# RWKV-7 recurrence and GELU MLP: the first five chunks as an explicit order of small steps, one PSUM place per product, and 64x128 tiles in three more chunks

## The chip, the cores and the metric
The kernel runs on one core of a Trainium2 chip. The metric is the device time of one execution in microseconds (us). Five engines work side by side, each through its own instructions in order: TensorE (PE in the profile; its weight loads are PEld), VectorE (DVE), ScalarE (ACT), GpSimd (POOL) and SyncE (SP), which only issues DMAs. DMAs are issued on the queues of SyncE (SPq), ScalarE (ACTq) and GpSimd (POOLq).

## The reference
A recurrence over 768 steps, for 4 batches and 8 heads with a 40 x 40 state each, feeds a two-layer MLP with the exact GELU over all 3072 tokens:

```python
for t in range(S):                                   # S = 768, D = 40
    kt, vt, rt = (k[:, :, t], v[:, :, t], r[:, :, t])
    wt, at, bt = (w[:, :, t], a[:, :, t], b[:, :, t])
    y[:, :, t] = np.einsum('bhd,bhde->bhe', rt, state)
    Sa = np.einsum('bhde,bhe->bhd', state, at)
    state = (state * wt[:, :, None, :] - np.einsum('bhd,bhe->bhde', Sa, bt)
             + np.einsum('bhd,bhe->bhde', vt, kt))

x = y.transpose(0, 2, 1, 3).reshape(B * S, H * D)    # 3072 x 320
h = x @ w_in                                         # 320 x 2048
g = 0.5 * h * (1.0 + erf(h * inv_sqrt2))
out = g @ w_out                                      # 2048 x 320
```

The two weights reach the kernel as 64-bit floats, and are made into 32-bit floats on the chip.

## The kernel before
**The recurrence in chunks.** The 768 steps are cut into 12 chunks of 64. Inside a chunk the recurrence is solved with matrix products. A chunk c goes through these functions (the tile names are those of the profile): `logs`, `sums` and `turn_w` make the running decays (tiles wT, cum); `turn_a`, `turn_b`, `turn_k`, `turn_v`, `turn_r` transpose the inputs on TensorE, and `scale_a`, `scale_b`, `scale_k` apply the decays. `make_N` multiplies the scaled a and b (N_ps) and masks the product into N, `make_A` and `make_RV` do the same for their products. The unit triangular matrix of N is inverted. Then X is what the state gives (`make_X`), sa what the chunk's steps write back (`make_saT`, `make_sa`, tile SM), M and QY the two parts of the output (`make_M`, `make_y2`, `make_QY`), xt the chunk's 128-row input to the MLP (`outputs`), and `new_state` makes the next state.

**The inverse** of chunk 0 is found by repeated squares on TensorE (`squares`, five of them). From chunk 1 on it goes through GpSimd: `make_N` stores the 32 x 32 blocks of N to DRAM with four DMAs on SyncE, `start_inverse` loads them as Nb with two, its 31 column steps (two instructions each, L759 and L761, or st/spare_x in chunk 1, W/tmp from chunk 2 on) eliminate, `store_inverse` writes the blocks back, `fetch_inverse` loads them as Tt and T2. `turn_corner` transposes one of them, `corner` makes the off-diagonal product J and copies it to Js, `joined` makes the second product (J too in the profile) and copies it into Tt. From chunk 5 on Nb comes from a transpose on VectorE (`turn_N`) instead of DRAM.

**The MLP.** `mlp(c)` is a generator of pieces. Eight products "ph" (two in each of four PSUM tiles; L1167) multiply xt with w_in, a GELU on ScalarE moves each PSUM tile into gt (L1169), and "po" multiplies gt with w_out: plainly for chunks 0 to 2 (L1178), with seven products of half the size in place of eight from chunk 3 on (`seven`, L1098). A ph product goes in 64x64 tiles or, for chunks 3 to 8, in 64x128 tiles.

**Weights.** `first_load(False, part)` brings a quarter of the raw w_in words (1.05 MB), `first_load(True, part)` the last rows of a half (0.52 MB), `second_load(f, ...)` a sixteenth of w_out (0.33 MB). The conversion of a piece (`to_float`, in generator form, 10 for w_in and 16 for w_out) is some eight instructions over VectorE, ScalarE and GpSimd or VectorE. `convert(n)` issues the first half of n pieces and the second half of the pieces begun before.

**Order.** The schedule is written out by hand: the order of the source lines is the order in which each engine issues. For the first chunks it is a list of calls (L1227 to L1485), then a loop `for c in range(3, NCH)` in which `fill()` places the next piece of an MLP between the steps of the recurrence. A call such as `make_N(c)` there issues its matmuls, and its mask or copy right behind them. PSUM is four places of two banks ("duo0" to "duo3"); `places` gives each product its place in the order of the calls. `keep(n, ...)` puts n columns of 128 (ident times the mask cum_m) in front of the next product, as work that only keeps TensorE busy; a call replaces what an earlier one asked for and no product has taken yet, and so 12 such columns are issued. `unused(tile, eng)` fills the unused rows of an input tile with a constant before its load.

```python
    ("ph", "123322000100030003000300030003000300030003001302"),
    ...
def duo(name):
    pt = psum.tile([P, 2, 512], FP32, tag="duo" + next(places[name]), name=name, bufs=1)
    while asked:
        n = asked.pop()
        mm(pt[:, 0, :n * P], ident, cum_m.unsqueeze(1).to_broadcast([P, n, P]))
    return pt
```

Of the kernel before, what the change touches and what calls it, by code (L numbers as in the profile page):

```python
# [20 lines left out]
def kernel(  # L21
# [49 lines left out]
    P = 128  # L71
# [22 lines left out]
    def keep(*columns):  # L94
# [3 lines left out]
    places = {n: iter(x) for n, x in (  # L98
        ("warm", "0"),
        ("wT_ps", "30112"),  # L100
        ("cum", "22031"),
        ("aT_ps", "200"),
        ("nT_ps", "0313"),
        ("N_ps", "310322222222"),
        ("sq", "20332"),
        ("kT_ps", "1033"),
        ("A_ps", "312000000000"),
        ("vT_ps", "012"),
        ("rT_ps", "122"),
        ("RV_ps", "020111111111"),  # L110
        ("J", "133022222222"),
        ("av", "310010000000"),
        ("QY", "200121212323232323232323"),
        ("J2", "213322222222"),
        ("sap", "333"),
        ("saT_ps", "200321111111"),
        ("M_ps", "023311111111"),
        ("X", "20211111111"),
        ("tn_ps", "32"),
        ("ph", "123322000100030003000300030003000300030003001302"),  # L120
        ("po", "133130313031303130313031303130313021302"),
    )}
# [124 lines left out]
    def load_VR(c):  # L247
        VR = turned_in.setdefault(c, {})["VR"] = VR_ring()
        for e in range(2):
            nc.sync.dma_start(out=VR[half(e)].rearrange("p g q m d -> p (g q m) d")[:, :, :D], in_=rows_of(v, c, e))  # L250
# [20 lines left out]
    st_ring = ring("st", 1, [P, 2, NP, G, HP], lambda t: t.rearrange("p e i g d -> p (e i g) d")[:, :, D:], nc.gpsimd)  # L271
    SM_ring = ring("SM", 1, [P, 2, G, NP, VC], None, None)
    early_b = work.tile([P, NK, TB], FP32, tag="xt", name="early_b").rearrange("p k t -> p (k t)")
    early_w = SM_ring().rearrange("p e g n c -> p (e g n c)")[:, :G * DM + REST]
# [76 lines left out]
    def to_float(dst, words, eng):  # L351


        n = words.shape[1] // 2
        lo, hi = (words.rearrange("p (n x) -> p n x", x=2)[:, :, x] for x in range(2))
        both = work.tile([P, LW], UINT32, tag="conv", name="conv", bufs=2)
        power, mant = both[:, :n], both[:, LW // 2:LW // 2 + n]
        nc.vector.tensor_scalar(power, hi, 0x7FF00000, None, ALU.bitwise_and)  # L358
        nc.scalar.activation(power, power, ACT.Relu, bias=rebias, scale=8.0)  # L359
        nc.vector.tensor_scalar(mant, hi, 0x000FFFFF, 0x00100000, ALU.bitwise_and, ALU.bitwise_or)  # L360
        if eng is nc.vector:
            yield
        nc.vector.scalar_tensor_tensor(power, hi, 0x80000000, power, ALU.bitwise_and, ALU.bitwise_or)
        mant_f, power_f, lo_f = mant.bitcast(FP32), power.bitcast(FP32), lo.bitcast(FP32)
        if eng is nc.vector:
            eng.scalar_tensor_tensor(mant_f, lo, 2.0 ** -32, mant, ALU.mult, ALU.add)
            eng.scalar_tensor_tensor(dst, mant_f, 2.0 ** -20, power_f, ALU.mult, ALU.mult)
        else:
            nc.scalar.mul(lo_f, lo, 2.0 ** -52)
            nc.scalar.mul(mant_f, mant, 2.0 ** -20)  # L370
            eng.tensor_tensor(mant_f, mant_f, lo_f, ALU.add)
            eng.tensor_tensor(dst, mant_f, power_f, ALU.mult)
        yield

    queue, begun = [], []

    def convert(n, last=False):

        for _ in range(n):
            begun.append(queue.pop(0))  # L380
            next(begun[-1], None)
            if len(begun) > 1:
                next(begun.pop(0), None)
        if last:
            while begun:
                next(begun.pop(0), None)
# [40 lines left out]
    def first_convert(kt, part, eng):  # L427
        if wide_in:
            w = LW // 2
            yield from to_float(w_in_sb[:, kt, part * w:(part + 1) * w], first_raw.pop((kt, part)), eng)  # L430

# [13 lines left out]
    def second_convert(f, eng):  # L445
        if wide_out:
            yield from to_float(w_out_sb[:, f], second_raw.pop(f), eng)

    def first_pieces(kts, part, eng):
        queue.extend(first_convert(kt, part, eng) for kt in kts)  # L450

    def second_pieces(engs):
        queue.extend(second_convert(f, {"v": nc.vector, "g": nc.gpsimd}[e]) for f, e in enumerate(engs))
# [6 lines left out]
    decays, turned_in = {}, {}  # L460
# [5 lines left out]
    def sums(c):  # L466
        logw = raws.pop((c, "w"))
        pt = duo("wT_ps").rearrange("p e (n t) -> p e n t", t=C)
# [5 lines left out]
        cum = duo("cum")[:, :, :DM]  # L474
# [4 lines left out]
        wp = wp_ring()  # L479
        turned_in.setdefault(c, {})["wp"] = wp  # L480
        if c < NB:
            nc.scalar.activation(wp[:, :, 1:].rearrange("p (n e) t -> p e n t", e=2), pt, ACT.Exp)  # L482
        else:
            en = turned_in.setdefault(c, {})["en"] = by_batch(side("en", "kT", 1))
            for to, scale_ in ((wp[:, :, 1:].rearrange("p (g n e) t -> p g e n t", g=G, e=2), 1.0),
                               (en.rearrange("p (e g n) t -> p g e n t", e=2, g=G), -1.0)):
                for g in range(G):
                    nc.scalar.activation(to[:, g], pt[:, ::1 - 2 * g, g * NP:(g + 1) * NP], ACT.Exp, scale=scale_)
        rw = (avs_ring if c in (1, 2) else part_ring)()[:, :, :DM]
# [3 lines left out]
    def turn_w(c):  # L493
        wp = turned_in.setdefault(c, {})["wp"] = wp_of[(c - NB - 1) % 3]
# [28 lines left out]
    def flip(src, name):  # L523

        pt = duo(name).rearrange("p g (n t) -> p g n t", n=NP)
# [21 lines left out]
    def turn_a(c):  # L547
        if c < NT:
            turned_in.setdefault(c, {})["a_ps"] = flip(by_pair(raws.pop((c, "a"))), "aT_ps")
            return  # L550
        aT = turned_in.setdefault(c, {})["aT"] = work.tile([P, 2, G, NP, C], FP32, tag="aT", name="aT", bufs=2)
# [33 lines left out]
    def turn_b(c):  # L585
        t = turned_in[c]
        nT = side("nT", "nT", 1)
        if c >= NB:
            nT = by_batch(nT)
# [4 lines left out]
        nc.scalar.copy(nT, flip(by_pair(t["nb"]), "nT_ps"))  # L594
# [8 lines left out]
    def turn_k(c):  # L603
        t = turned_in[c]
        if c >= NB:
            kT = t["k_turned"] = by_batch(side("k_turned", "conv", 2))
            turn(kT, c, "k_turned")
            return
        kT = side("kT", "kT", 1)
        nc.scalar.copy(kT, flip(by_pair(t["ks"]), "kT_ps"))  # L610
# [8 lines left out]
    def turn_v(c):  # L619
        t = turned_in[c]  # L620
        vT = side("vT", "late", 1)
        if c < NT:
            pt = duo("vT_ps").rearrange("p q (m t) -> p q m t", m=NP)
            for q in range(2):
                for m in range(NP):
                    for g in range(G):
                        mm(pt[half(g), q, m], t["VR"][:, g, q, m, :HP], ident)
            nc.scalar.copy(vT, pt)
        else:
            turn(vT.rearrange("p q m (e t) -> p (q m e) t", e=2), c, "v")  # L630
        t["vT"] = parts(vT)

    def turn_r(c):
        rT = side("rT", "rT", 2)
        if c < NT:
            raw = raws.pop((c, "r"))
            nc.scalar.copy(rT, flip(lambda q, m: raw[:, NP * q + m].rearrange("p g d -> p (g d)"), "rT_ps"))
        else:
            turn(rT.rearrange("p q m (e t) -> p (q m e) t", e=2), c, "r")
# [11 lines left out]
    def products(name, lT, rT, swap):  # L651

        pt = duo(name).rearrange("p j (g n t) -> p j g n t", g=G, n=NP)
# [18 lines left out]
    def make_N(c):  # L672
# [9 lines left out]
        masked(flat(N), products("N_ps", t["nT"], t["aT"], True))  # L682
        if c > NB:
            for q in (1, 3):
                rows = slice(q * BL, (q + 1) * BL)
                nc.scalar.copy(flat(N)[rows, :, :BL], flat(N)[rows, :, BL:])  # L686
        if c in direct or c > NB:
            return
# [8 lines left out]
    def make_RV(c, mask=True):  # L697
        t = turned_in[c]
        t["RV_ps"] = products("RV_ps", t["vT"], t["rT"], False)
        if mask:  # L700
            mask_RV(c)

    def mask_RV(c):
# [4 lines left out]
        else:  # L708
            nc.scalar.copy(to, t.pop("RV_ps"))
            nc.gpsimd.tensor_tensor(to, to, upper.unsqueeze(1).to_broadcast([P, 2 * G * NP, C]), ALU.mult)  # L710

    def make_A(c, mask=True):
        t = turned_in[c]
        t["A"] = work.tile([P, 2, G, NP, C], FP32, tag="nT", name="A")
        t["A_ps"] = products("A_ps", t["kT"], t["aT"], False)
        if mask:
            mask_A(c)
# [5 lines left out]
    def make_av(c):  # L723
        t = turned_in[c]
        av = duo("av")[:, :, :G * NP * D].rearrange("p x (g i d) -> p x g i d", g=G, i=NP)
        for g, i, x, e, q, m in units():
            mm(av[half(e ^ x), x, g, i], t["A"][half(e), x, g, i], t["VR"][half(e), g, q, m, :D])
        avs = t["avs"] = avs_ring()
        nc.scalar.copy(avs[:, :, :DM], av.rearrange("p x g i d -> p x (g i d)"))
# [4 lines left out]
    def start_inverse(c, eng, place=None):  # L734
# [10 lines left out]
        for y in range(2 if c > NB else 0):  # L745
            eng.tensor_copy(W.rearrange("p s t -> p (s t)")[:, y::BL + 2][:, :BL // 2],
# [934 lines left out]
```

## Time and profile before

| | |
|---|---|
| runs, us | 673.82, 674.12, 674.56 |
| span of the profiled execution, us | 673.1 |
| granted TensorE clock over the span | 0.964 |
| PE busy | 634.4 us, 94% of the span, 14602 matmuls |
| PEld busy | 550.9 us, 82% |
| DVE busy | 430.0 us, 64% |
| POOL busy | 403.9 us, 60% |
| ACT busy | 329.8 us, 49% |
| DMA | 70.11 MB, 104 GB/s on average |

The span runs from the first to the last recorded instruction of one execution; the profile gives no other time for that execution, and its span lies 1.0 us under the median of the runs. A PE row such as "101.27 4.48 PE L1167 MATMUL ph<-xt,w_in_sb 64*64 64x256 f32 x77" in the time-ordered view reads: start at 101.27 us, 4.48 us long, 77 matmuls of line 1167 in 64x64 tiles over 256 columns. A bracket behind it gives the idle time before it and what ended it. The slices are 16.8 us long.

### The profile page before, as it was taken

How to read it: one execution, taken by the hardware profiler on the slowest of the kernel's cores; microseconds unless marked ns; L12 is line 12 of the kernel's file. 1: busy time of each engine (PE TensorE's matmuls, PEld its weight loads, DVE VectorE, ACT ScalarE, POOL GpSimd, SP SyncE). 2: the span in 40 equal slices, each digit the busy share in tenths (PEclk: the TensorE clock that was granted, in tenths of full speed). 3: DMA queues.
4: the chain of work that ended last, by engine and by line, in shares of the span. 5: the costliest groups of instructions: out<-in, count | busy, mean ns of one | idle time of the engine just before them, and what ended most of it. 6: DMA issues, size and time to landing. Idle time of an engine off the chain costs nothing.

```text
span 673.1 us, 32696 instructions
## 1 busy us (share of the span) xinstructions
PE 634.4 (94%) x14602; PEld 550.9 (82%) x14602; DVE 430.0 (64%) x571; ACT 329.8 (49%) x637; POOL 403.9 (60%) x835
## 2 busy tenths in 40 slices
PE   7668888879999999999999999999999999999997
PEld 4557767666777787899899899898998998989977
DVE  2322869996435596787887887696887865623303
ACT  5223565362332562673772855845737728344020
POOL 5648327870581586876886877868868868720000
PEclk9785789899999999999999999999999999999999
DMA  9777747946745855726748648557457471220100
GB/s 136 140 147 124 125 90 181 186 82 127 150 97 99 155 111 98 132 60 112 131 88 134 127 79 135 117 93 151 99 96 137 93 124 42 50 50 4 41 2 21
DMA packets 270607, 70.11 MB, mean 104 GB/s; under 512 B 251003, under 2 KB 267675, under 8 KB 270466
## 3 DMA queue, kind: packets, MB, share of 16 engines
q1 hardware_dynamic: 265146, 62.10, 49.9%
q0 software_dynamic: 1680, 4.07, 3.4%
q8 instruction: 115, 1.88, 1.2%
q10 hardware_dynamic: 3640, 1.84, 1.1%
q14 instruction: 26, 0.21, 0.1%
HBM read 56.16 MB, written 7.86 MB: 95 GB/s over the span
## 4 chain that ended last, share of the span: by engine, by line
PE 80%; DVE 9%; POOL 4%; issue 2%; ACT 2%; DMA 1%; ACTq 1%; SPq 0%; DVEq 0%; POOLq 0%
PE ph L1167 28%; PE po L1098 21%; PE po L1178 8%; PE QY L138 6%; PE J L138 2%; PE X L138 2%; POOL st L761 2%; POOL st L759 2%; PE A_ps L138 2%; PE N_ps L138 1%; PE saT_ps L138 1%; PE av L138 1%; PE RV_ps L138 1%; PE M_ps L138 1%; PE sq L138 1%
## 5 line engine op out<-in xcount | busy, mean ns | idle before, releaser
L1167 PE MATMUL ph<-xt,w_in_sb 64*64 64x256 f32 (+1 forms) x2896 | 218.3, 377 | 1.3 <-ACT gt L1169 1.2
L1167 PEld LDWEIGHTS ph<-xt,w_in_sb 64*64 64x64 f32 (+1 forms) x2896 | 170.4, 151 | 33.5 <-ACT gt L1169 1.9
L759 POOL TENSOR_TENSOR tmp<-W,Nb 128x126 f32<-128x126 f32 (+22 forms) x310 | 130.3, 420 | 62.1 <-DMA Nb<-N 39.1
L761 POOL TENSOR_TENSOR W<-W,tmp 128x126 f32<-128x126 f32 (+22 forms) x310 | 140.5, 453 | 24.3
L1098 PE MATMUL po<-w_out_sb,gt 128*128 128x160 f32 x576 | 82.7, 302 | 0.3 <-issue 0.3
L1098 PEld LDWEIGHTS po<-w_out_sb,gt 128*128 128x128 f32 x576 | 78.8, 190 | 1.7 <-issue 0.6
L1169 ACT ACTIVATE gt<-ph 128x1024 f32<-128x1024 f32 x48 | 49.2, 1024 | 43.3 <-PE ph L1167 42.7
L1066 ACT COPY turned<-within 32x256 f32<-32x256 f32 (+3 forms) x144 | 46.4, 322 | 26.3 <-DVE within L1055 24.5
L1178 PE MATMUL po<-w_out_sb,gt 128*128 128x320 f32 x192 | 55.8, 448 | 2.2 <-ACT wpT L482 2.2
L1178 PEld LDWEIGHTS po<-w_out_sb,gt 128*128 128x128 f32 x192 | 36.7, 195 | 17.4 <-ACT wpT L482 2.4
L961 ACT COPY SM<-sa 32x64 f32<-32x64 f32 (+1 forms) x108 | 31.9, 295 | 14.0 <-DVE sa L955 12.4
L521 ACT COPY part<-part 32x256 f32<-32x256 f32 (+1 forms) x112 | 36.1, 322 | 1.5
L1102 DVE TENSOR_TENSOR os<-os,po 128x160 f32<-128x160 f32 x63 | 20.0, 318 | 24.0 <-PE po L1098 20.9
L359 ACT ACTIVATE conv<-conv,rebias 128x320 uint32<-128x320 uint32 (+1 forms) x26 | 16.1, 624 | 35.3 <-DVE conv L358 28.7
L886 ACT COPY Js<-J 128x256 f32<-128x256 f32 x11 | 4.1, 371 | 56.6 <-PE J L138 56.6
L710 POOL TENSOR_TENSOR VR<-VR,upper 128x1024 f32<-128x1024 f32 x8 | 19.0, 2370 | 17.8 <-DMA Tt<-inv 11.1
L955 DVE STREAM_TRANSPOSE sa<-saT 128x1024 f32<-128x1024 f32 x9 | 11.2, 1242 | 26.3 <-ACT saT L945 26.3
L1098 PE MATMUL po<-extra,half 128*128 128x160 f32 x176 | 26.1, 303 | 0.0
L686 ACT COPY N<-N 32x512 f32<-32x512 f32 x14 | 8.6, 616 | 34.8 <-DVE N L649 34.7
L1098 PEld LDWEIGHTS po<-extra,half 128*128 128x128 f32 x176 | 24.2, 190 | 0.3
L1118 DVE TENSOR_TENSOR half<-gt 128x1024 f32<-128x1024 f32 x9 | 11.4, 1265 | 18.3 <-ACT gt L1169 18.3
L1011 DVE TENSOR_TENSOR xt<-QY,wpT 128x512 f32<-128x512 f32 x18 | 11.5, 682 | 16.9 <-PE QY L138 16.9
(257 smaller groups left out, 1203.2 us busy)
## 6 DMA issues: line engine op xcount, KB each, us to landing
VR<-in_v_dram SPq DMA_DIRECT2D x24, 160.0 KB
out_dram<-os SPq DMA_DIRECT2D x46, 80.0 KB
b_rows<-in_b_dram SPq DMA_DIRECT2D x22, 160.0 KB
k_rows<-in_k_dram SPq DMA_DIRECT2D x22, 160.0 KB
Tt<-inv SPq DMA_DIRECT2D x44, 64.0 KB
a_pairs<-in_a_dram SPq DMA_DIRECT2D x18, 144.0 KB
v_pairs<-in_v_dram SPq DMA_DIRECT2D x36, 72.0 KB
r_pairs<-in_r_dram SPq DMA_DIRECT2D x36, 72.0 KB
```

The lines of the kernel that those rows point to most:

```text
L138: nc.tensor.matmul(o, lhsT, rhs, start=first, stop=True, skip_group_check=True)
L521: nc.scalar.copy(to[at:at + BL, :, x, z * BL:end], tmp[on:on + BL, e, :, q * BL:q * BL + end - z * BL])
L710: nc.gpsimd.tensor_tensor(to, to, upper.unsqueeze(1).to_broadcast([P, 2 * G * NP, C]), ALU.mult)
L759: eng.tensor_tensor(t, W[:, :rows, j:j + 1].to_broadcast([P, rows, rest]), Nb[:, j:j + 1, j + 1:].to_broadcast([P, rows, rest]), ALU.mult)
L761: eng.tensor_tensor(W[:, :rows, j + 1:], W[:, :rows, j + 1:], t, ALU.add)
L961: copy(t["SM"][to:to + BL, g].rearrange("p q m c -> p (q m) c")[:, :, d * BL:end], t["sa"][at:at + BL, :, to:to + end - d * BL])
L1066: nc.scalar.copy(tn[to:to + deep, :, at:at + wide], within[0][at:at + deep, :, to:to + wide])
L1098: nc.tensor.matmul(po[:, n, :DM // 2], l_[:, f], r_[:, f], start=f == 0, stop=f == NF // 2 - 1)
L1102: nc.vector.tensor_tensor(to, one_, other, ALU.add)
L1167: nc.tensor.matmul(ph[to:end, x, s, g], w_in_sb[half(x), kt, p * P + to:p * P + end], xt[half(x), kt, g], start=kt == 0, stop=kt == NK - 1)
L1169: nc.scalar.activation(gt[:, 4 * q:4 * q + 4].rearrange("p (x s) t -> p x s t", x=2), ph, ACT.Gelu)
L1178: nc.tensor.matmul(po[:, g], gt[:, f, g * P:(g + 1) * P], w_out_sb[:, f], start=f == 0, stop=f == NF - 1)
```

## The change
It rewrites how the first five chunks are ordered, and three details.

- Functions that issued matmuls and the copies or masks behind them are cut into parts that are called one by one: `make_N`, `mask_N`, `store_N`; `start_inverse`, `load_Nb`, `substitute` (n column steps); `flip_v`, `copy_v` and the like; `corner`, `copy_corner`; `joined`, `copy_joined`; `make_X`, `add_X`; `square(k)`, `turn_square(k)`; `scale_y`, `move_y`; `ph`, `gelu`, `po`, `put` for the MLP. A conversion becomes a `Unit` with the steps a, r, m, b, s, g, each for one engine (a, m, b on VectorE, r and s on ScalarE, g on GpSimd).
- The order of chunks 0 to 4 is one long list of such steps; the loop begins at c = 5 and there takes the same steps in the same order as before.
- `duo(name, at)` takes the PSUM place by the chunk or product, no longer by the order of calls, and the table is a new one for the first chunks.
- 72 columns of `keep` are issued in place of 12.
- ph goes in 64x128 tiles in chunks 0 to 8. In chunk 2 one product was split into column halves; it no longer is.
- The w_out loads that were issued on ScalarE's queue (3, 4, 8, 9, 11) are issued on SyncE's.
- The state's tile (st) and SM become single tiles instead of rings where they were ones of one.

```diff
-    def duo(name):
-        pt = psum.tile([P, 2, 512], FP32, tag="duo" + next(places[name]), name=name, bufs=1)
+    def duo(name, at):
+        pt = psum.tile([P, 2, 512], FP32, tag="duo" + places[name][at], name=name, bufs=1)
...
-        ("N_ps", "310322222222"),
+        ("N_ps", "203132022222"),
...
-        ("ph", "123322000100030003000300030003000300030003001302"),
+        ("ph", "122200013020032201000100030003000300030003001302"),
...
+    class Unit:
+        def a(self):
...
+            nc.vector.tensor_scalar(self.power, self.hi, 0x7FF00000, None, ALU.bitwise_and)
+        def r(self):
+            nc.scalar.activation(self.power, self.power, ACT.Relu, bias=rebias, scale=8.0)
+        def m(self):
+            nc.vector.tensor_scalar(self.mant, self.hi, 0x000FFFFF, 0x00100000, ALU.bitwise_and, ALU.bitwise_or)
...
+    def substitute(c, n=BL):
+        run(islice(steps_of[c], n))
...
-                        for to, end in ((0, P),) if NS <= c < NCH - 3 and q in (0,1,2,3,) else ((0, HP), (HP, P)):
+                for to, end in ((0, P),) if c in wide_chunks else ((0, HP), (HP, P)):
...
+    phs, pos, wide_chunks = {}, {}, range(NCH - 3)
```

The list around the three steps that the prediction follows. Chunk 1 before, from the store of N (inside `make_N(1)`) to the load of Nb (inside `start_inverse(1)`), and after:

```diff
-    make_N(1)
-    scale_k(0)
...
-    first_load(False, 0, early(0, 4), eng=nc.gpsimd)
-    run(zero)
-    run(start_inverse(1, nc.gpsimd, (spare_x[:, :BL * BL], spare_w[:, :nw], spare_w[:, nw:])))
...
-    first_load(True, 0, early(4), eng=nc.sync)
-    corner_direct(0, (nc.scalar, nc.scalar, nc.scalar, nc.scalar))
-    make_av(0)
-    first_load(False, 1, eng=nc.sync)
+    first_load(False, 0, early(0, 4), eng=nc.gpsimd)
+    first_load(False, 1, eng=nc.sync)
+    keep(1, 4)
+    make_N(1)
+    mask_N(1)
+    load_VR(1)
+    keep(1, 4)
+    square(1)
+    mask_A(0)
+    store_N(1)
+    U[0].a()
...
+    turn_square(1)
...
+    first_load(True, 1, spare_raw[:, :LW], eng=nc.sync)
...
+    start_inverse(1, nc.gpsimd, (spare_x[:, :BL * BL], spare_w[:, :nw], spare_w[:, nw:]))
+    load_Nb(1)
+    substitute(1, 8)
```

From chunk 1's corner to chunk 2's column steps:

```diff
-    corner(1)
...
-    make_X(1)
...
-    joined(1)
...
-    make_sa(1)
...
-    make_N(2)
-    convert(1)
-    convert(1)
-    fill()
-    run(start_inverse(2, nc.gpsimd))
-    for n in "av": unused(paired[n], nc.gpsimd, 1.0)
+    make_X(1)
...
+    turn_corner(1)
+    corner(1)
...
+    joined(1)
+    copy_joined(1)
...
+    make_N(2)
+    mask_N(2)
+    store_N(2)
+    ph(0, 0)
...
+    load_Nb(2)
+    load_w(3)
...
+    load_a(3)
...
+    unused(paired['a'], nc.gpsimd, 1.0)
+    logs(3)
+    substitute(2, 8)
```

Around chunk 2's corner and joined, which stands behind them on TensorE:

```diff
-    corner(2)
-    load_v(3)
-    fill()
...
-    turn_b(3)
-    make_X(2)
-    make_N(3)
-    seconds(1, (14, 14), last=True)
-    run(start_inverse(3, nc.gpsimd))
-    load_r(3)
-    joined(2)
+    po(0, 0, 0)
...
+    make_X(2)
...
+    po(0, 1, 0)
...
+    make_N(3)
...
+    corner(2)
+    copy_corner(2)
+    keep(2)
+    joined(2)
+    copy_joined(2)
+    mask_N(3)
```

More of the change, by code (lines that the diff above doesn't have):

```diff
@@ L1190 @@
-    pieces = []
-    def fill(n=1):
-        while n and pieces:
-            if next(pieces[0], "end") == "end":
-                pieces.pop(0)
-            else:
-                n -= 1
-    def load_next(c):
-        load_w(c)
-        load_a(c)
-    def seconds(n, *loads, last=False):
-        convert(n, last)
-        for load in loads:
-            second_load(*load)
+            ph(c, q)
+            gelu(c, q)
+            yield
+        yield from seven(c)
+    sevens = {c: seven(c) for c in (3,)}
@@ new lines @@
+    turn_w(6)
+    load_a(6)
+    turn_corner(4)
+    put(2, 0)
+    corner(4)
+    load_VR(5)
+    copy_corner(4)
+    store_inverse(5, (nc.gpsimd,))
+    make_X(4)
+    weight_sums(1)
+    joined(4)
+    gelu(3, 2)
+    turn_blocks(range(0, 8))
+    put(2, 1)
+    turn_k(5)
+    turn_part(5, ())
+    ph(3, 3)
+    copy_joined(4)
+    add_X(4)
+    keep(1)
+    make_saT(4)
+    copy_saT(4)
+    gelu(3, 3)
+    start_inverse(6, nc.gpsimd)
+    ph(3, 1)
+    gelu(3, 1)
+    substitute(5, 8)
+    substitute(5, 8)
@@ L1563 @@
[L1563 to L1565 removed]
             if more2:
                 turn_r(n2)
[L1568 to L1570 removed]
                 scale_a(n2)
[L1572 to L1573 removed]
+            else:
+                scale_kT(n)
+        next(pieces)
+        if more:
             turn_part(n, range(10, 16))
             scale_b(n, nc.gpsimd)
[L1576 removed]
+            substitute(n)
```

1480 lines of the change are left out of this document (893 added, 587 removed).

## The prediction
> **What bounds the kernel now.** I read the page's slices first, then busy time by stretch, then the time-ordered rows of TensorE, of SyncE's DMA queue and of GpSimd around the first three chunks. The slices:
>
> ```profile
> PE   7668888879999999999999999999999999999997
> PEclk9785789899999999999999999999999999999999
> ```
>
> Left of slice 10 (168 us) TensorE is neither full nor at full clock; right of it there is nothing to win except by doing less work. Busy time by stretch (us, then TensorE, weight loads, VectorE, ScalarE, GpSimd, granted clock, DMA share, GB/s):
>
> ```profile
> 0.00:40.00 40.00, 27.13 (x754) 20.73 (x757) 11.72 (x14) 15.07 (x17) 19.09 (x49) 0.91 0.84 138
> 40.00:80.00 40.00, 32.87 (x979) 29.65 (x972) 18.60 (x24) 16.58 (x24) 27.51 (x66) 0.66 0.71 126
> 80.00:120.00 40.00, 33.37 (x1000) 29.47 (x999) 31.16 (x44) 22.83 (x32) 19.71 (x28) 0.90 0.65 144
> 120.00:160.00 40.00, 33.98 (x645) 25.36 (x638) 35.72 (x69) 18.14 (x25) 25.53 (x58) 0.93 0.68 135
> 160.00:200.00 40.00, 38.62 (x947) 29.87 (x945) 17.12 (x32) 13.73 (x17) 21.56 (x57) 1.00 0.61 123
> ```
>
> TensorE idles 32.7 us up to 160 and 1.4 us up to 200. Its busy time below full clock (27.13 x 0.09 + 32.87 x 0.34 + 33.37 x 0.10 + 33.98 x 0.07) is 19 us more. So 53 us is all that a new order can ever win. TensorE's rows show where the loss ends:
>
> ```profile
> 101.27 4.48 PE L1167 MATMUL ph<-xt,w_in_sb 64*64 64x256 f32 x77
> ...
> 154.43 0.75 PE L138 MATMUL J<-L,N 32*32 32x32 f32 x64
> 155.11 4.57 PE L1178 MATMUL po<-w_out_sb,gt 128*128 128x320 f32 x16
> ...
> 161.66 1.16 PE L138 MATMUL N_ps<-aT,nT 40*64 40x64 f32 x64
> 164.17 0.22 PE L138 MATMUL J<-Tt,Js 32*32 32x32 f32 x2 [1.35 <-DVE N L649]
> ```
>
> The last row is joined(2), the third chunk's second inverse product. Behind it TensorE never waits again for more than 0.7 us. In the changed order the same products stand ahead of joined(2): four ph of chunk 0, two of its four po, X(2), N(3). So the forecast is: when does joined(2) start, and how much TensorE work is added behind it?
>
> **The chain to joined(2).** It runs through two rounds of the same kind: N is masked, stored to DRAM, loaded as Nb, eliminated column by column on GpSimd, stored, fetched, then corner and joined. GpSimd's first and last column product of chunks 1 and 2:
>
> ```profile
> 40.48 0.23 POOL L759 TENSOR_TENSOR st<-st,spare_x 128x31 f32<-128x31 f32 x1 [11.83 <-PE A_ps L138]
> ...
> 67.89 0.23 POOL L761 TENSOR_TENSOR st<-st 128x16 f32<-128x16 f32 x1
> ...
> 113.62 0.38 POOL L759 TENSOR_TENSOR tmp<-W,Nb 128x31 f32<-128x31 f32 x1
> ...
> 145.03 0.29 POOL L761 TENSOR_TENSOR W<-W,tmp 128x16 f32<-128x16 f32 x1
> ```
>
> and SyncE's queue around chunk 1:
>
> ```profile
> 27.91 1.97 SPq L693 DMA_DIRECT2D N<-N  x4
> 34.35 1.14 SPq L750 DMA_DIRECT2D spare_x<-N  x2
> ...
> 68.14 1.27 SPq L785 DMA_DIRECT2D inv<-st  x2
> 71.91 3.30 SPq L798 DMA_DIRECT2D Tt<-inv  x4
> ```
>
> **Chunk 1, GpSimd start: 5.5 us later.** first_load(False,1) (1.05 MB) and VR(1) (0.33) move ahead of the store of N(1), first_load(True,1) (0.52) between it and the load of Nb, while first_load(False,0) runs on GpSimd's queue as before. Up to Nb's last byte the queues must move nine inputs of 0.33, 2 x 1.05, 0.33, 0.26 (N), 0.52, 0.52 (Nb): 6.68 MB. Before moved 5.5 MB in 40 us (138 GB/s); 1.16 MB more at the 158 GB/s of 40 to 50 us end at 47.3. Between 30 and 40 us before moved 122 GB/s, waiting for this very round trip; filling that takes off 2.3 us. So 45 to 47, taken 46, against 40.5. From below: if N isn't held up, 40.5. From above, as rival two: the slices' lowest early rate, 125 GB/s, gives 53.
>
> 27.6 us of columns (40.48 to 68.12) then end at 73.8. VectorE's new work beside them could stretch this to chunk 2's 31.7 us; I take 27.6, because VectorE waits most of this time for chunk 0's squares, and keep the 4 us for the range.
>
> **Chunk 1 to N(2): 4 us earlier.** Store to corner(1) took 13.3 us (68.14 to 81.42), so corner(1) is at 87. Behind it stand, by their rows: J 0.75, its copy 0.4, joined 0.7, cum 1.3, RV 1.1, aT 1.0, nT 0.95, saT 1.1, N 1.1 and nine warming columns at 0.28 (the 128x512 pair of "sap" took 1.12): 11 us, so ph of chunk 0 starts at 98 against 101.2. SyncE agrees: from the store 8.4 us to the end of the fetch, then a second_load 0.95, a(2) 1.4, b(2) 1.3, the eleven moves of y (8 by the rows from 82.56) and another second_load end at 95, 2 us before the moves land. Before had corner at 81.4 but then lost 2.9 us to conversions ahead of add_X(1) and put kT, wT, tn and more in front. N(2) is masked at 99.2, against 103.0.
>
> **Chunk 2's round: 0.8 us later, yet joined(2) 8 us earlier.** 103.0 to the first column was 10.6 us, which gives 109.8. But unused(a) now stands ahead of the columns on GpSimd, and it waits for load_a(3), which SyncE issues behind k(2), r(2), N, a second_load, Nb and w(3): 110, landed 113.5, plus 0.92 us memset: 114.4. 31.7 us of columns and 9.1 us to corner(2) (145.32 to 154.43): 155.2; J and its copy: joined(2) at 156.2, against 164.17. Before had po, nT, X and N (155.11 to 162.8) between corner and joined; the change puts them ahead of corner(2), under GpSimd's columns.
>
> That needs TensorE there by 155. From 98: 4 ph x 4.5, sap, y2, M, QY 2.9, vT, kT, wT, A, cum, rT, av, RV, tn at about 1.1 each, two po x 4.4, X, nT, N: 47 us, plus 2.5 us waiting for VectorE (the eight w_out conversions U10 to U17 end near 138; before they ended at 144.9, begun 8 us later): 147.5. 7.5 us to spare, which is also the price limit: a slip under it costs nothing.
>
> **Chunk 0 and warming, taken at nothing.** U[0].a stands ahead of turn_square(1) on VectorE and waits for 2.1 MB of w_in, to about 36; the squares, masks and copies behind it wait too. Chunk 0's QY then ends near 68 (before 79.4); its state is wanted by X(1), just after corner(1) at 87, and the cover is that wait for GpSimd. Past it each us counts. The 57 more warming columns ahead of joined(2) (16 us) lie in the same waits.
>
> **Behind joined(2): +2.3 us.** 64x128 tiles in chunks 1 and 2 (chunk 0's lie in the spare time). Three starts of X bracket one chunk with such tiles and one without:
>
> ```profile
> 504.58 1.14 PE L138 MATMUL X<-st,aT 40*64 40x40 f32 x64
> ...
> 551.11 1.14 PE L138 MATMUL X<-st,aT 40*64 40x40 f32 x64
> ...
> 595.85 1.14 PE L138 MATMUL X<-st,aT 40*64 40x40 f32 x64
> ```
>
> 46.53 less the N product (0.98) that the second lacks is 45.55, against 44.74: the wide tile costs 0.2 us a product, 1.6 for eight. Three warming columns 0.8; the dropped split -0.1. The third inverse: N(3)'s store waits on SyncE behind VR(3), k(3), r(3) and three second_loads, to 167; columns 174.4 to 204.6; turned at 212.5, where TensorE arrives at 217; the second fetch lands 222, joined(3) is due at 223. That costs nothing, with 1 us of cover; then each us counts. From chunk 5's loop on the order is as it was.
>
> **Sum.** -8.0 + 1.6 + 0.8 - 0.1 = -5.7: span 673.1 becomes 667.4. The runs' median, 674.12, lies 1.0 above the span: 668.
>
> [...] Chunk 2's columns took 31.7 us beside a VectorE busy 28.5 of 30 us (110 to 140), chunk 1's 27.6 beside 9.6 of 30: contention costs 4 us at full load. [...]
>
> **The rivals.**
> One: N(1)'s round trip is not delayed; the 0.61 DMA share of 30 to 40 us leaves room, and the queues may share better than by bytes. All steps come 5.5 us sooner, and load_a(3) with them: 662, down to 657 if that landing also gains. Against it: the bytes.
> Two, the slower side: the weight loads hold N(1) longer, on SyncE and on the engines, and what follows is one for one. At 53 us for Nb the gain is gone and 1.3 us more: 675.5 is passed; at 57, 679. For it: DMA share is already 0.84 and 1.04 in single 10 us stretches. Against: w_in's long rows moved fastest.
> [...]
> Four: the order does what it says and the 1 us of cover at joined(3), or the PSUM places, give 5 us back: 673.
>
> **How the numbers follow.** Forecast 0.46 (664 to 672), one 0.23, two 0.17, three 0.05, four 0.09. This kernel's measurement tells about 0.2% (1.3 us) from no change. Faster 0.69, same 0.09, slower 0.22. The range 657 to 679 takes one's lower end and two at 57.
>
> **What would show it.** Right: Nb(1)'s first column near 46; ph's first row near 98; joined(2) near 156 with TensorE idle just before corner(2); behind it 2.3 us more TensorE time. Wrong: a first column past 53, joined(2) waiting on VectorE, or new TensorE gaps right of 200 us.

## The result, and the profile after
Slower by 1.0%: 682.69 us median (681.15 to 685.22, four runs) against 674.34 (673.82 to 678.52, four runs) before; ratio 1.0103, 95% interval 1.0063 to 1.0144. The profiled execution's span is 680.4 us, 7.3 more than before. The forecast was 668, its range 657 to 679; the result lies above it. It ended on the side of rival two, but not by its mechanism: the weight loads held chunk 1's round less than forecast (first column at 44.63 us, forecast 46).

The slices of the changed kernel, TensorE's row and its granted clock:

```profile
PE   8779899889999969999999999999999999999997
PEclk9998999998999979999999999999999999999999
```

The lost clock of the first ten slices is mostly gone. Something else stands there that before had not: counted from 0, slice 14 (17.01 us each, so 238 to 255 us) has a 6 for TensorE with a 7 for the clock under it, in the part that was full before. The forecast's checkpoints, from the same views as in the prediction, first TensorE, then GpSimd's first column products of chunks 1 and 2:

```profile
95.39 2.78 PE L1267 MATMUL ph<-xt,w_in_sb 64*128 64x256 f32 x18
...
153.54 0.26 PE L139 MATMUL J<-Tt,Js 32*32 32x32 f32 x2
...
217.07 0.75 PE L139 MATMUL J<-L,N 32*32 32x32 f32 x64
...
223.34 0.22 PE L139 MATMUL J<-Tt,Js 32*32 32x32 f32 x2
```

```profile
44.63 0.23 POOL L833 TENSOR_TENSOR st<-st,spare_x 128x31 f32<-128x31 f32 x1 [13.84 <-DMA spare_x<-N]
112.86 0.24 POOL L833 TENSOR_TENSOR tmp<-W,Nb 128x31 f32<-128x31 f32 x1 [5.06 <-DMA Nb<-N]
```

| step | before | forecast | after |
|---|---|---|---|
| chunk 1's first column (GpSimd) | 40.48 | 46 | 44.63 |
| first ph of chunk 0 | 101.27 | 98 | 95.39 |
| chunk 2's first column | 113.62 | 114.4 | 112.86 |
| joined(2) | 164.17 | 156.2 | 153.54 |
| corner(3) | 222.17 | 217 | 217.07 |
| joined(3) | 228.28 | 223 | 223.34 |
| X(5) | 318.24 | 312.5 | 322.41 |
| span | 673.1 | 667.4 | 680.4 |

X(5)'s forecast is the time before less the 5.7 us of the sum. "X(3) to X(4)" below is the time from the start of X in chunk 3 to its start in chunk 4.

At 223 us the forecast stood, in part because two misses cancelled (see below). From X(3) (222.86 before, 217.75 after) to the end it is 450.2 us before and 462.7 after: 12.4 us are lost there, 7.8 of them between X(3) and X(4) (48.57 us before, 60.86 after, of which 4.51 are a ph of chunk 3 that the new order takes in). TensorE's rows there, before (A(4) runs without a wait) and after:

```profile
246.72 1.61 PE L138 MATMUL QY<-VR,extra 64*64 64x104 f32 x64
248.15 0.75 PE L138 MATMUL A_ps<-aT,en 40*64 40x64 f32 x37
```

```profile
236.23 4.59 PE L1267 MATMUL ph<-xt,w_in_sb 64*128 64x256 f32 x40
246.01 1.98 PE L139 MATMUL A_ps<-aT,en 40*64 40x64 f32 x64 [5.20 <-DVE SM L706]
247.78 3.00 PE L139 MATMUL QY<-SM,extra 64*64 64x104 f32 x64
250.55 2.01 PE L139 MATMUL QY<-VR,extra 64*64 64x104 f32 x64
```

A(4) waits 5.20 us for VectorE's mask of M(3), whose PSUM place it takes. Behind the wait the three products take 6.99 us where the same ones take 4.38 at full clock: 2.6 us more. VectorE's rows and SyncE's show why the mask is late:

```profile
232.19 1.25 DVE L217 STREAM_TRANSPOSE shared<-a_pairs 128x1024 f32<-128x1024 f32 x1 [7.36 <-DMA a_pairs<-in_w_dram]
...
233.51 3.02 DVE L521 TENSOR_TENSOR_SCAN shared<-shared,starts 128x260 f32<-128x260 f32 x4
238.06 1.25 DVE L217 STREAM_TRANSPOSE aT<-a_pairs 128x1024 f32<-128x1024 f32 x1 [1.53 <-DMA a_pairs<-in_a_dram]
...
244.73 1.23 DVE L706 TENSOR_TENSOR SM<-M_ps,upper 128x1024 f32<-128x1024 f32 x1
```

```profile
219.12 2.93 SPq L757 DMA_DIRECT2D N<-N  x4
...
227.39 2.25 SPq L212 DMA_DIRECT2D a_pairs<-in_w_dram  x4
```

turn_w(5) stands ahead of the mask on VectorE and waits 7.36 us for w(5). SyncE issues that load at 227.39, as the last of a row of DMAs at 0.5 to 1.0 us each (chunk 2's moves, VR(4), chunk 3's fetches, N(4), Nb(4), chunk 1's outputs). M(3)'s product itself was ready at 236.3.

Half clock, in this case's rows: granted 1.00 up to 244.5 us, 0.50 from 244.6 to 251.2 and 1.00 again from 251.4, though TensorE idled only from 240.8 to 246.0. The fall comes 3.7 us after the idle time began, and the clock is back 5.4 us after the idle time ended.

The rest of the 12.4: 1.5 us from X(4) to X(5) (two warming columns of 0.41 and 0.42 at saT(4) and A(5), and a stall of 0.44), 1.8 from X(5) to X(6) (ph of chunk 4 waits 1.20 for xt(4)), 1.3 behind.

### The profile page after: what moved, and what is told of

It reads as the page before. It is cut to its first block, busy times and chain, and to the rows that moved or that the text cites. A ratio compares the mean times of both kernels' runs of the same rounds, so it can differ in the third digit from the quotient of the medians.

```text
span 680.4 us, 31815 instructions
## 1 busy us (share of the span) xinstructions
PE 644.5 (95%) x14172; PEld 558.1 (82%) x14172; DVE 419.5 (62%) x571; ACT 331.0 (49%) x638; POOL 405.1 (60%) x835
## 4 chain that ended last, share of the span: by engine, by line
PE 60%; POOL 8%; SPq 8%; DMA 5%; DVE 3%; issue 2%; ACT 0%; DVEq 0%; POOLq 0%
PE ph L1267 22%; PE po L1203 18%; PE QY L139 6%; POOL tmp L833 4%; POOL W L835 4%; PE po L1277 4%; PE J L139 2%; SPq L1129 1%; PE A_ps L139 1%; PE saT_ps L139 1%; PE av L139 1%; DMA N<-N 1%; PE N_ps L139 1%; PE M_ps L139 1%; PE RV_ps L139 1%
## 5 line engine op out<-in xcount | busy, mean ns | idle before, releaser
L1267 PE MATMUL ph<-xt,w_in_sb 64*128 64x256 f32 (+1 forms) x2400 | 223.5, 382 | 2.4 <-DMA xt<-xt 2.0
L1267 PEld LDWEIGHTS ph<-xt,w_in_sb 64*128 64x128 f32 (+1 forms) x2400 | 179.6, 166 | 30.9 <-issue 3.2
L833 POOL TENSOR_TENSOR tmp<-W,Nb 128x126 f32<-128x126 f32 (+22 forms) x310 | 128.0, 413 | 74.7 <-DMA Nb<-N 51.4
L835 POOL TENSOR_TENSOR W<-W,tmp 128x126 f32<-128x126 f32 (+22 forms) x310 | 142.6, 460 | 24.3
L1277 PE MATMUL po<-w_out_sb,gt 128*128 128x320 f32 x192 | 54.1, 437 | 0.0
L367 ACT ACTIVATE conv<-conv,rebias 128x320 uint32<-128x320 uint32 (+1 forms) x26 | 15.6, 621 | 17.5 <-DVE conv L364 17.4
L706 DVE TENSOR_TENSOR SM<-M_ps,upper 128x1024 f32<-128x1024 f32 x12 | 14.7, 1223 | 13.8 <-PE M_ps L139 13.6
```

The source lines that it names most:

```text
L833: eng.tensor_tensor(t, W[:, :rows, j:j + 1].to_broadcast([P, rows, rest]), Nb[:, j:j + 1, j + 1:].to_broadcast([P, rows, rest]), ALU.mult)
L835: eng.tensor_tensor(W[:, :rows, j + 1:], W[:, :rows, j + 1:], t, ALU.add)
L1267: nc.tensor.matmul(pt[to:end, x, s], w_in_sb[half(x), kt, p * P + to:p * P + end], xt[half(x), kt], start=kt == 0, stop=kt == NK - 1)
L1277: nc.tensor.matmul(pos[c][:, g], gt[:, f, g * P:(g + 1) * P], w_out_sb[:, f], start=f == 0, stop=f == NF - 1)
```

## The experiments
The theory after the two traces: behind joined(2) VectorE stands in order behind loads that SyncE issues late, TensorE waits for a mask behind them, and its clock falls. Rivals: the 64x128 tiles or the warming columns are the loss, or the rounds of the inverses take back whatever is gained. Positions are of the profiled execution, ratios against the kernel before.

**VectorE's order alone.**

```diff
-    turn_a(5)
...
-    scale_a(5)
...
     mask_M(3)
+    turn_a(5)
+    scale_a(5)
```

> The changed kernel with two calls moved: turn_a(5) and scale_a(5) stand behind mask_M(3) on VectorE. Theory: the 5.2 us that TensorE idles ahead of A(4) are VectorE's queue, in which the mask of M(3) stands behind transposes that wait for chunk 5's loads, and the half clock for 6 us behind it (2.6 us) is its consequence. In front of the mask then stand only turn_w(5) (ends 236.5), scale_kT (1.2), the transpose and copies of sa (3.0) and the mask (1.2): it ends near 242 in place of 245.9, the idle time falls from 5.2 to about 1.3 us, the clock does not fall, and the span from 680.4 to 674 to 676. Rival: the chunk's inverse on GpSimd sets corner(4) (277.9) and takes it back: 679 to 681 although the idle time at A(4) is gone. Second rival, the 64x128 tiles and the warming columns are the loss: no change.

The mask ended at 241.3 (expected near 242), and A(4) ran at 241.33 without a wait. The span was 681.2, the ratio 1.0095 (1.0060 to 1.0130). TensorE, then VectorE:

```profile
250.09 7.01 PE L1277 MATMUL po<-w_out_sb,gt 128*128 128x320 f32 x16 [4.75 <-DVE A L706]
```

```profile
247.68 1.25 DVE L217 STREAM_TRANSPOSE vT<-v_pairs 128x1024 f32<-128x1024 f32 x1 [4.00 <-DMA v_pairs<-in_v_dram]
248.85 1.19 DVE L706 TENSOR_TENSOR A<-A_ps,upper 128x1024 f32<-128x1024 f32 x1
```

The wait moved by one load: turn_v(4) waits for v(4), the mask of A(4) stands behind it, po of chunk 2 has A(4)'s place, and behind its wait it takes 7.01 us, against 4.57 at full clock. X(3) to X(4) stayed at 60.8 us. The rival that I named for no gain, the inverse's round, was not the cause: the wait at po is VectorE's.

**SyncE's order too.** store_N(4) moves to right behind mask_N(4), then:

```diff
     fetch_inverse(3, (1, 2))
+    start_inverse(4, nc.gpsimd)
+    load_Nb(4)
+    load_w(5)
+    load_VR(4)
```

> As the kernel before it, and on SyncE's queue the store of N(4) goes ahead of the last two fetches of chunk 3's inverse, the load of Nb(4) right behind them, then w(5), then VR(4) and chunk 1's outputs. Theory: SyncE issues one DMA per half microsecond and is never free from 201 to 250 us, so that place in its queue is time: Nb(4)'s first column product moves from 229.1 to about 226, w(5) lands at about 226.5 in place of 232.2, the mask of M(3) ends at about 238.5, TensorE does not idle at A(4), and corner(4) can be as early as 270: span 671 to 673, some 3 us less than with VectorE's order alone. Rival: the wait at A(4) has another cause (a copy on ScalarE, the PSUM place): no less than with VectorE's order alone.

X(3) to X(4) fell from 60.9 to 54.6 us, and po's wait to 1.09: 6.3 of the 7.8 us are explained by the two orders. Nb(4)'s first column came at 227.2. (SyncE is not issuing all the time up to 250, nor always a DMA per half microsecond: after the change the rows from 199 to 252 us give 0.49 to 1.23 us each, and it stood idle from 229.64 to 233.46, since the load of a(5) takes the tile that turn_w(5) reads until 233.44.) The span was 678.5 and the ratio 1.0067 (1.0037 to 1.0098), less than hoped: this execution had X(3) 2.0 us later, in a part that the edit does not touch, and lost 1.2 between X(4) and X(5).

**The mask of A(4) first.** As the one above, and:

```diff
     make_A(4)
+    mask_A(4)
     turn_v(4)
     undecay(5)
-    mask_A(4)
```

> As e2_sp_order, and mask_A(4) stands ahead of turn_v(4) on VectorE. In the run with VectorE's order alone the wait did not go, it moved: the mask of A(4) stood behind turn_v(4), which waited 4.0 us for v(4)'s load, and po of chunk 2, which takes A(4)'s PSUM place, waited 4.75 us; in e2_sp_order 1.1 us of it was left. Theory: this last 1.1 us goes and no other takes its place, so that X(3) to X(4) is 53.5 us (60.9 after the change, 54.6 in e2_sp_order), and the span is 674 to 677. Rival: the next load in VectorE's queue takes over, X(3) to X(4) stays at 54.6 or more.

Both waits are gone; the largest that is left between X(3) and X(4) is 0.52 us:

```profile
243.55 1.16 PE L139 MATMUL A_ps<-aT,en 40*64 40x64 f32 x64
...
247.49 4.57 PE L1277 MATMUL po<-w_out_sb,gt 128*128 128x320 f32 x16
```

X(3) to X(4) is 54.6, as with SyncE's order, so the rival's figure held: a wait of 0.52 for xt(3) ahead of chunk 3's first ph and one of 0.32 at av(4) took over. X(3) to X(5) is 98.7 against 104.7 after the change. The ratio is 1.0033 (0.9997 to 1.0068): no longer shown slower than the kernel before. The span, 679.2, missed what was expected, for X(3) came at 220.3, 2.6 us later than in the changed kernel's trace. That part came 0.1 to 2.6 us later in the three kernels so far without an edit in it, and TensorE's stalls for which the profile shows no wait vary there too: 10.6 us in all before 100 us in the changed kernel's trace, 12.1 here, 14.2 in the kernel with SyncE's order.

**Work under GpSimd's columns.** In the changed kernel, po(0, 0, 0) and po(0, 1, 0) move from ahead of corner(2) to behind copy_joined(2).

> The changed kernel with two po of chunk 0 (8.9 us of TensorE) moved from ahead of corner(2) to behind joined(2). Theory of the prediction, which the trace after bears out up to 223 us: GpSimd's columns set corner(2), and what TensorE does under them is free. Then corner(2) stays within 2 us of 151.7, TensorE idles some 9 us more ahead of it, and X(3), 217.8 after the change, comes 9 us later, at 226 to 228. Rival: corner(2) follows TensorE, and moves forward when work ahead of it goes: corner(2) near 143, X(3) unchanged.

```profile
153.02 1.08 PE L139 MATMUL J<-L,N 32*32 32x32 f32 x64 [3.63 <-DVE L L959]
```

corner(2) stayed (153.02 for 151.71) and X(3) came at 227.0, 9.2 us later than after the change; from 130 to 152 us TensorE was busy 13.9 us in place of 20.2. The one execution took 697.41 us. The mechanism of the prediction's gain, work put ahead of a joined(2) that GpSimd sets, is shown. The cover is thin, though: TensorE waited only 1.77 us for corner(2) after the change, and not at all in the kernels with SyncE's order and with the mask of A(4) first, where corner(2) came at 154.0 and 156.2.

**The tiles, undone.** `wide_chunks = range(3, NCH - 3)`.

> The changed kernel with 64x64 tiles for ph in chunks 0 to 2, as before. Theory: chunk 1's four ph took 19.9 us behind joined(2), of which 1.9 are half clock, against 17.4 before: 0.7 us a chunk, and chunks 1 and 2 lie behind joined(2): 1.4 us less, span 679.0. Prediction's term: 1.6 less, 678.8. Rival, the tiles are the loss: 7 us less, 673.4.

Slower still, span 689.9, ratio 1.0216 (1.0175 to 1.0258), against all that was expected. GpSimd's columns of chunk 2 began 4.3 us later (117.1) and of chunk 3 6.5 later (179.5), w(5) was issued at 234.3 in place of 227.4, and A(4) waited 10.37 us. Here the slip ahead of joined(2) is paid twice, once itself and once through SyncE's queue at A(4). It says nothing of the tile's own price.

**No warming columns.** `keep` asks for none.

> The changed kernel with no warming columns at all. Theory: the granted clock from 40 to 80 us falls from 0.91 towards the 0.66 of before, the products of chunk 0 and 1 take longer, but joined(2) (153.5) is set by the round of the inverse through SyncE and GpSimd and comes at most 3 us later; behind joined(2) six columns (1.5 us) are gone: span 679 to 682. Rival: the warming is what brought joined(2) forward by 10.6 us: joined(2) near 160, span 685 or more. Second rival: the columns are the loss, they stand in TensorE's way: 672 or less.

Span 686.6, ratio 1.0115 (1.0053 to 1.0176). The clock from 50 to 60 us fell from 0.83 to 0.55; joined(2) came at 155.4, 1.9 us later than after the change, and X(3) at 218.8, only 1.0 later. Most of the rest is A(4)'s wait, 7.46 us for 5.20, and a stall of 1.85 at joined(4). So the warming is neither the gain at joined(2) nor the loss.

**Taking more of the loss away.** As with the mask of A(4) first, and: 64x64 tiles in chunks 1 and 2, no warming column at cum(4), saT(4) and A(5), `move_y(4, (1,))` right behind `move_y(4, (0,))`.

> As e7_mask_A_first, and three terms of the sum behind joined(2) taken away: 64x64 tiles for ph in chunks 1 and 2 (0.17 us a product by the rows, 1.4 us), three warming columns at cum(4), saT(4) and A(5) (1.2 us), and the second half of xt(4)'s moves ahead of the weight loads on SyncE (the wait of 1.2 us at 327 us). Theory: 3.8 us less than e7_mask_A_first: 670 to 673, faster than the kernel before by a little. Rival: what is taken away there comes back as waits for chunk 3's and 4's inverses, which SyncE and GpSimd set: no less than e7_mask_A_first.

And with first_load(True, 1) behind load_Nb(1):

> As e8_all, and first_load(True, 1), eight DMAs that SyncE issued from 34.0 to 40.0 us, stands behind the load of Nb(1) in place of ahead of it. Theory: the first column of chunk 1 comes 4 us earlier (44.6 to about 41), and joined(2) by 2 to 4 us; behind joined(2) TensorE is full, so the span falls by as much: 667 to 671. Rival: chunk 2's round waits for its own loads and conversions (the a(3) and w_out loads on SyncE), joined(2) stays, and the span too.

Spans 688.7 and 679.6, ratios 1.0142 (1.0057 to 1.0227) and 1.0140 (1.0036 to 1.0244); the second's profiled execution is the quickest of four (681.3 to 689.2 us). X(3) came at 224.2 in the first. In the second the earlier load did what was asked (first column at 41.65, joined(2) at 151.2, X(3) at 215.2), but X(3) to X(5) was 109.2 and 108.3 us against 98.7. VectorE in the second:

```profile
312.57 0.71 DVE L959 STREAM_TRANSPOSE L<-Tt 128x512 f32<-128x512 f32 x1 [3.97 <-DMA Tt<-inv]
313.21 1.18 DVE L1236 TENSOR_TENSOR gt<-gt,SM 128x1024 f32<-128x1024 f32 x1
```

The six DMAs of xt(4) had pushed Tt back on SyncE, turn_corner(5) waited, and po behind the subtraction waited 3.05 us: the same mechanism a third time. A fourth is hidden under "issue", which means that the profile shows nothing that TensorE waited for. In the second again:

```profile
245.30 1.25 DVE L217 STREAM_TRANSPOSE vT<-v_pairs 128x1024 f32<-128x1024 f32 x1 [4.52 <-DMA v_pairs<-in_v_dram]
...
249.05 0.47 DVE L1142 TENSOR_TENSOR st<-QY,st 128x320 f32<-128x320 f32 x1
```

```profile
249.62 1.41 PE L139 MATMUL av<-VR,A 64*64 64x40 f32 x64 [2.86 <-issue]
```

av(4) has the PSUM place of QY(3)'s first half (duo2 in `places`), and L1142 in new_state(3) is that half's last reader; on VectorE it stands behind turn_v(4), which waits for v(4)'s load. av(4) starts 0.10 to 0.11 us after L1142 ends, in all six kernels that have the mask of A(4) first, with idle times of 0.32 to 3.75 us (3.23 in the first of these two). The stall of 1.8 at joined(4) is of another kind (see below).

**Those moves with the corner put right.** The mask of A(4) first, first_load(True, 1) behind load_Nb(1), xt(4)'s moves early, turn_corner(5) behind the third piece of chunk 3's seven; tiles and warming as after the change.

> As e7_mask_A_first, with two moves of e8_all and e9_all_load kept, each with what it pushed aside put right: first_load(True, 1) behind the load of Nb(1) (first column at 41.6 us in e9_all_load, 44.6 after the change); the second half of xt(4)'s moves ahead on SyncE (the wait ahead of ph of chunk 4 went, X(5) to X(6) 47.0 in place of 48.6 us), and turn_corner(5) behind the third piece of chunk 3's seven, since in e9_all_load it waited 4.0 us on VectorE for Tt, which those moves had pushed back, and po behind it 3.05 us. Warming columns and 64x128 tiles as after the change. Theory, every wait behind joined(2) is VectorE standing in order behind a load that SyncE issued late: X(3) at 214 to 217, X(3) to X(4) 53.5 to 54.7, X(4) to X(5) 43.5 to 44.5, X(5) to X(6) 47, span 671 to 674, level with the kernel before or just under it. Rival: the waits in e8_all and e9_all_load came from the missing warming columns or the narrow tiles, and the moves bring nothing: 677 to 680, as e7_mask_A_first.

The first column came at 43.29, and X(3) at 218.9, later than expected (214 to 217). X(3) to X(5) was 99.2 us, close to the theory, but X(5) to X(6) 52.6: ph waited 1.65 us for a GELU, corner(6) 2.67 for its transpose on VectorE. Both go back to loads again: the GELU stands on ScalarE behind copies of a transpose that VectorE makes behind turn_k(6), which waited 3.95 us for its load, and the transpose of corner(6) waited 4.47 us for Tt. Span 681.4, ratio 1.0101 (1.0065 to 1.0138). The moves bring nothing, and not by the rival's cause.

**xt(4) by another queue.** The mask of A(4) first, `move_y(4, (1,), nc.scalar)`, no warming column at cum(4), saT(4), A(5).

> As e7_mask_A_first, with the second half of xt(4)'s moves issued on ScalarE's queue in place of SyncE's, so that nothing on SyncE is pushed back, and without the three warming columns at cum(4), saT(4) and A(5). In e7_mask_A_first ph of chunk 4 waited 0.75 us for xt(4) and ran at half clock behind that (6.28 us in place of 4.5). Theory: X(5) to X(6) 47 us in place of 49.7, X(3) to X(5) 97.5 in place of 98.7, span 675, level with the kernel before. Rival: ScalarE is held by seven more issues, its copies come late, and a new wait stands there: 679 as e7_mask_A_first, or more.

X(5) to X(6) was 47.9, 1.7 less than with the mask of A(4) first. X(3) to X(5) was 102.1, with 2.52 of idle time at av(4), VectorE's L1142 again, and a stall of 1.30 at A(5): span 680.1, ratio 1.0067 (1.0033 to 1.0102). No version beat the kernel before.

**The tile by itself.** With the mask of A(4) first, 64x64 tiles in chunks 1 and 2:

> As e7_mask_A_first, with 64x64 tiles for ph in chunks 1 and 2. In e3_narrow the tiles could not be read, since X(3) came 4.3 us later and the wait at A(4) grew from 5.2 to 10.4 us with it. Theory (the rows): 0.17 us a product, the two chunks 1.4 us faster, 675 to 678. Rival: 320 more matmuls in these chunks stall TensorE where it waits for nothing that the profile shows (in e8_all 3.2 and 1.8 us, with such tiles): 2 to 5 us slower than e7_mask_A_first.

And the kernel before with 64x128 tiles in chunks 0 to 2:

> The kernel before with 64x128 tiles for ph in chunks 0 to 2, this part of the change alone. Prediction's term: 0.2 us a product, 1.6 us for the chunks behind joined(2); by the rows after, 1.4: 0.2% slower than before, span 674.5. Rival: fewer matmuls, fewer stalls of TensorE's instructions in the first 160 us, where before idled 32.7 us: 2 us faster or more, span 671.

The first: 683.4, ratio 1.0103 (1.0060 to 1.0146), the rival's size but not its cause: 3.75 us of idle time at av(4) are VectorE's L1142 (X(3) came 2.9 us sooner than with the mask of A(4) first, v(4)'s load did not), and only the stall of 1.64 at joined(4) is one without a wait. The second: 680.2, 1.0081 (1.0045 to 1.0116), slower by far more than the rows of the tile. Narrow tiles lose in one order, wide ones in the other. In the second, X(3) to X(4), with chunk 2's ph in it, is 48.6 us as in the kernel before: the tile costs nearly nothing there. The loss lies from X(2) to X(3), 68.2 us against 62.4:

```profile
209.49 0.55 PE L138 MATMUL av<-VR,A 64*64 64x40 f32 x21 [1.38 <-issue]
...
217.51 1.34 PE L138 MATMUL RV_ps<-rT,vT 40*64 40x64 f32 x37 [1.44 <-issue]
```

Counted in matmul records, the two stalls are 128 apart (21, 16, 64 and 27 of them), as in the first 60 us of every trace here, where they come 126 to 128 apart or a multiple of that. The pages have as many weight loads as matmuls (14602 of each before, 14172 after), so the step is some 256 instructions. The profile's pages have a queue with packets of 16 KB (packets, MB, share of 16 engines), before and after:

```profile
q8 instruction: 115, 1.88, 1.2%
```

```profile
q8 instruction: 111, 1.82, 1.1%
```

TensorE's matmuls and weight loads, 29204 before and 28344 after, are 114.1 and 110.7 times 256. The 15 traces have 204 idle times over 0.15 us ahead of a matmul that are put down to "issue": 198 end 2.2 to 3.8 us after the start of such a packet, the two above 2.5 and 2.3 us, and the six others are the av(4) ones. That TensorE stands there because its next instructions have not arrived is my reading of these numbers; no row shows it. To see if it is the place or the tile:

```diff
     for n in range(3):
         mm(pt[:, n % 2], w_in_sb[:, 0, :P], w_in_sb[:, 0, :512])
+    for n in range(32):
+        mm(pt[:32, 0, :32], w_in_sb[:32, 0, :32], w_in_sb[:32, 0, :32])
```

> e12_before_wide with 32 small matmuls (32x32, some 1 us) more at the very start, where TensorE waits for its first inputs; they write a PSUM place that is overwritten. Theory, the stalls at av(3) and RV(3) in e12_before_wide (1.4 us each, and half clock behind them) come from where TensorE's instruction stream is cut: all stalls move by 64 matmul records, the two at 209 and 218 us go or change size, X(2) to X(3) falls from 68.2 towards 63 to 65 us, the span from 680.2 to 674 to 677. Rival, the 64x128 tiles themselves make the stalls: X(2) to X(3) stays at 67 to 69, the span at 679 to 682.

Both stalls were gone, and X(2) to X(3) was 64.8: with 64 records more ahead of them and the same tiles they do not come, so it is the place in the instruction stream, not the tile. Of the 2.4 us that are left over the kernel before, 1.7 are the first ph, which took 6.28 us in place of 4.5, and 0.7 the rows of the tile. The span did not fall (681.5, ratio 1.0062, 1.0033 to 1.0092): the stalls of this kind had grown to 12.1 us before 100 us, from 7.9, and X(2) came 3.1 us later. Each of these kernels has one trace, so how far the lengths vary between executions of one kernel is not shown.

## Why the prediction was wrong
**Chunk 1's first column, 46 (44.63).** Right within its range, in part by luck: the working was by bytes, and the trace after shows that the two DMAs of Nb were issued at 39.99, when SyncE had done with the eight issues of first_load(True, 1) (33.99 to 39.95): the queue's order, not only the bytes. With that load behind Nb the first column came at 41.65 and 43.29 in two kernels; with it ahead, at 44.63 to 47.73 in the changed kernel and eight others that keep its order there.

**Chunk 1 to N(2), chunk 2's round.** ph at 95.39 for 98, chunk 2's first column at 112.86 for 114.4; it waited for Nb, not for the memset of unused(a) as I had it (done at 108). joined(2) came 10.6 us earlier in place of 8.0. The sum up to here held, and its mechanism is shown. Of the "7.5 us to spare" that TensorE was to have ahead of corner(2), 1.77 were left.

**The third inverse.** Due at joined(3) 223, TensorE at corner(3) 217: 223.34 and 217.07, no wait. That it is right to half a microsecond is luck: joined(2) came 2.7 us sooner than forecast, and the stretch from there to corner(3) took 63.5 us in place of 60.8.

**Behind joined(2): +2.3 us.** This is the step that failed: 18.0 us (from joined(2) to the end 508.9 before, 526.9 after). It counted the tiles, three warming columns and one inverse round, and then went on "From chunk 5's loop on the order is as it was". Between joined(3) at 223 and that loop at 322 lie 100 us of the new list, in which loads, transposes and masks of chunks 3 to 5 are rearranged as much as in the first two chunks. I took TensorE as full there because before it was, and did not put VectorE's and SyncE's new rows beside it. So the term left out the waits that VectorE's order, behind loads that SyncE issues late, puts on TensorE. 5.2 us of wait at A(4), 2.6 of half clock behind it (granted 0.50), 1.2 at xt(4), 1.0 at saT(2) for chunk 0's outputs, 1.9 of half clock at the ph behind joined(2) (6.37 for 4.51, granted 0.50 from 154 to 158 us) are the larger terms. VectorE's and SyncE's orders mended together took 6.2 of the 7.8 us at A(4) away, and with them the ratio is 1.0033 in place of 1.0103.

**The tiles, 0.2 us a product.** By the rows 4.51 against 4.34, 0.17: the size was right. But the tile also halves the matmul records of a product (80 to 40 in the rows), and in the kernel before with this tile stalls of 1.38 and 1.44 us stood between X(2) and X(3), which went with 64 records more at the start: the place in the instruction stream is what the term left out.

**Rivals.** Four named "the 1 us of cover at joined(3), or the PSUM places": the place was A(4)'s, but the wait is that of the place's reader in its own queue, with a price of 7.8 in place of 5. Three (0.05), on VectorE's conversions beside chunk 1's columns: the columns took 27.5 us (44.63 to 72.17) against 27.6 before, with two conversions beside them (VectorE at 51.28 and 69.39), so what more of them would cost was not put to a test. The trace before shows a price in like rows: a column product over 128x110 took 0.38 to 0.40 us in chunk 1 and 0.39 to 0.55 in chunk 2, beside the busier VectorE. One and two did not occur.

**Open.** Why the stalls before 100 us differ from 7.9 to 17.5 us between kernels that differ little there. The traces show that each ends 2.2 to 3.8 us after the start of a packet of queue q8, and one pair of kernels that two of them went with 64 records more at the start; what sets their length was not tried. No kernel here has v(4)'s load early enough for av(4) at every pace of TensorE, so whether the order can beat the kernel before is open too.

## What to carry to other kernels
When an order is written out by hand for every engine, the forecast has to go through all of the new list, on every queue: for each PSUM place, ask what its last reader stands behind on its engine, and for each transpose that waits for a load, how many DMA issues stand ahead of that load. Here a wait that one move took away came up again at the next load in the same queue (5.20 us at A(4) became 4.75 at po); it took SyncE's and VectorE's order together to bring the largest that was left to 0.52, and av(4) still came up behind them. Idle time put down to "issue" is not yet idle time without a wait (six of 204 here had one): look up who read its PSUM place last, and when that ended. And a hole in TensorE's work had a price in half clock too: 5.2 us of idle time at A(4) cost 7.8.

## What the runs showed of the hardware
In the first 60 us of each of 15 traces TensorE stalled, without a wait that the profile shows, at steps of 126 to 128 matmul records or a multiple of that. The pages have as many weight loads as matmuls (14602 of each before, 14172 after). Over the whole of the 15 traces there are 198 such stalls, 0.15 to 3.86 us each, with 7.9 to 17.5 us in the first 100 us of a trace. Each of them ended 2.2 to 3.8 us after the start of a 16 KB packet of queue q8, which has 115 packets before and 111 after, for 114.1 and 110.7 times 256 matmuls and weight loads. Behind 100 us the stalls come to 0.9 us in the kernel before and 1.0 in the changed one (up to 5.2 us in other kernels); in the first 100 us to 7.9 and 10.6. And 32 small matmuls (64 records) more at the start took stalls of 1.38 and 1.44 us away 190 us later.
